# Chunked attention and a bilinear FFN on one core: x columns in token order, output stores of 128 rows, one output chunk in each slot, weight sums moved into later steps

## The chip, the core and the metric

The kernel runs on one core of one Trainium2 chip. The metric is the device time of one execution in microseconds (us); less is better. The kernel before takes 318.6 us, the median of three runs (318.14 to 318.9).

## What is computed

Attention inside chunks of 64 tokens, 8 batches of 8 heads with 576 tokens each and a head size of 64. Its result, 4608 tokens by 512 columns, is x. An FFN follows in which two products of x are multiplied with each other:

```
scores = scale * (q_c @ k_c^T)            # q_c: batch, head, chunk, 64, 64
attn   = exp(scores) / sum(exp(scores))
x      = (attn @ v_c), heads side by side # 4608 x 512
a = x @ w_a                               # w_a: 512 x 1536
b = x @ w_b                               # w_b: 512 x 1536
out = (a * b) @ w_out                     # w_out: 1536 x 512, out: 4608 x 512 float32
```

## The kernel before

**Tiling.** The 4608 tokens are 9 blocks of 512 (K = 0 to 8), each of two units of 256. A unit holds four chunks of 64 tokens in each of its heads. Attention of a unit consists of *scores* (PE L248, then the exponential E on ACT, L256), *sums* (PE L263 multiplies E with ones; ACT takes the logarithm ln, L273), *inverse* (ACT L282, an exponential of -ln) and *values* (PE L296, then DVE L305 multiplies by the inverse and writes fp16 columns of x into the tile xT of the block). q and k are loaded (SP; L188 for the first six units, L176 after, as for v), cast to bf16 (POOL L203) and transposed: units 0 to 5 on PE, with the copy L225 to SBUF on ACT and DVE, later units by DMA (L230).

Within a unit, values computes two tiles of 128 tokens' columns, `av[0]` and `av[1]`. Tile c holds chunk c of token group 0 and chunk c of token group 1. L305 writes tile c into 128 columns that lie together. So the columns of x, and with them the rows of every output tile, stand in the order chunk, group, token, and an output tile of 128 rows covers two runs of 64 tokens in `out` that lie 128 apart.

**Hidden layer.** *Block 0* takes 12 steps of 128 hidden columns for its 512 tokens: PE L355 forms b (bank pb) and a (bank pc or po), ACT L363 copies b to SBUF (tiles b_sb, u_sb, v_sb, c_sb in turn), DVE L364 multiplies the two into ab_sb. *Block 1* does the same in 24 half steps: twelve for unit 2's 256 columns, then twelve for unit 3's (0 to 23); here b goes to pa or pq. *Blocks 2 to 8* use Strassen's scheme in Winograd's form, seven products in place of eight. Each takes six steps (pieces i of 256 hidden columns); a product is four matmuls of 128 x 256 (PE L405). p1 goes into bank pa, ACT L423 copies it into a bank pb, p6 adds to this bank, ACT L416 copies it out as u_sb, p5 adds again, and ACT L416 copies it out as v_sb. p3 of a step, which adds to the same bank, is issued in the *next* step, behind that step's p1. p7 and p4 go to bank pc; DVE adds with L443 and L444 and multiplies with L455.

This needs sums of weights (`combine_w`, DVE L129, four parts for each of six pieces; the list `combos` holds parts 0 to 2 of all pieces, and part 3 overwrites wa, which the steps of block 1 still read), sums of x (`combine_x`, DVE L385, tiles s), sums of w_out (POOL L158) and sums of ab (`combine_ab`, L485, on POOL or DVE, tiles so).

**Output.** Blocks 0 and 1 multiply ab by w_out as it is (PE L605; tiles of 128 rows). Block 0's four tiles stand between half steps of block 1 (`out_0`). Each tile is read out of its bank by DVE L598. Blocks 2 to 8 use the seven products again (class `OutGroup`, PE L543): 14 **chunks** of six matmuls of 128 x 256, two for each product. The chunks of a block run during the next block: a step has two **slots**, one behind p1 and one behind p2, and the table `chunks` says how many run in each. Readouts are L555 to L570 on ACT and L576, L583, L587 on DVE, into tiles o_sb. L576 reads the last product's two chunks out of bank po. L583 and L587 read what the fifth product left.

For the last block two half groups `ends`, one for each half of the rows, run behind the last step's p3 and p4. Their products go in the order 0, 1, 2, 4, 3, 5, 6; their banks are given in a tuple, of which the third is that of the fifth and seventh products.

**Order.** The program's order of code is each engine's order of instructions; an engine runs its own in order and waits at each for the semaphores of others. SP issues loads, transposes and stores in one such queue. PSUM has eight banks: pa, pc, po and pq one each, pb and pt two each. `bank()` without a pool takes the next of the list `spread`. The pool of o_sb has two buffers. `store` (L487 to L491) issues each output tile of 128 rows as two DMAs of 64, on SP; for the last tiles, with `both`, one of the two goes to ACT's queue.

## Time and profile before

| what | us |
|---|---|
| median of three runs | 318.6 |
| the profiled execution, its own time | 317.81 |
| span of its trace | 316.0 |
| of it outside the span | 1.8 |

By stage, the busy time of the engines in the profiled execution, in us:

| stretch | length | PE | DVE | ACT | POOL | DMA share |
|---|---|---|---|---|---|---|
| 0 to 41.6: loads, first units, block 0 | 41.60 | 32.39 | 21.29 | 19.70 | 22.46 | 1.05 |
| 41.6 to 85: block 1 | 43.40 | 41.13 | 33.43 | 22.56 | 22.76 | 1.07 |
| 85 to 115: block 2 | 30.00 | 29.63 | 20.89 | 19.73 | 18.88 | 1.07 |
| 115 to 300: blocks 3 to 8 | 185.00 | 183.18 | 128.24 | 126.42 | 110.57 | 0.57 |

The mean granted clock of TensorE is 0.998. Times in rows of the trace are us from the start of the span. A row of the time order gives start, length, engine, line, operation, output <- inputs, and in brackets the idle time of the engine ahead of it with what ended it. A busy PE is not PE at its peak, since matmuls overlap and their ends are modelled: four matmuls of one product show 0.60, though the next product can start earlier. SPq is SP's queue of DMA issues.

### The profile page before, as it was taken

The numbers are of one execution on the slowest core, as the hardware profiler recorded it, in microseconds if no ns is written. First come the engines' busy times: TensorE is split into PE (matmuls) and PEld (weight loads), VectorE is DVE, ScalarE is ACT, GpSimd is POOL, SyncE is SP. The second block draws the span as 40 slices with busy tenths as digits, with TensorE's granted clock in tenths as the row PEclk, the third lists the DMA queues.
The fourth block names the chain that finished last, engine by engine and source line by source line (L and its number), as shares of the span: only waits on it lengthen the run. The fifth ranks groups of instructions, "written<-read, shape, count | busy, mean of one in ns | idle before, by whom it ended". The sixth has DMA issues, their size and how long they took to land.

```text
span 316.0 us, 8540 instructions
## 1 busy us (share of the span) xinstructions
PE 294.8 (93%) x3476; PEld 228.6 (72%) x3478; DVE 209.6 (66%) x346; ACT 191.8 (61%) x346; POOL 177.6 (56%) x168
## 2 busy tenths in 40 slices
PE   2879999998999999999999999999999999999981
PEld 1534477675576768787888788878887888788871
DVE  3356778965875776578657774877487748847651
ACT  1643666238466566767776668576857685564530
POOL 1575656632646869756945593659356604750830
PEclk9999999999999999999999999999999999999999
DMA  7999999999999984998279838982973002200415
GB/s 233 308 381 292 287 337 310 268 220 183 230 238 223 199 198 100 153 232 218 68 173 187 222 91 191 197 220 66 218 108 77 2 2 66 70 1 2 94 40 133
DMA packets 139495, 54.03 MB, mean 171 GB/s; under 512 B 114624, under 2 KB 133568, under 8 KB 139456
## 3 DMA queue, kind: packets, MB, share of 16 engines
q1 hardware_dynamic: 139296, 53.36, 72.9%
q8 instruction: 27, 0.44, 0.6%
q10 hardware_dynamic: 160, 0.13, 0.1%
q14 instruction: 12, 0.10, 0.1%
HBM read 37.75 MB, written 9.44 MB: 149 GB/s over the span
## 4 chain that ended last, share of the span: by engine, by line
PE 69%; DVE 7%; DMA 7%; POOL 5%; SPq 4%; ACT 4%; issue 3%; POOLq 0%; DVEq 0%; ACTq 0%
PE pb L405 16%; PE pc L405 10%; PE pa L405 9%; PE po L543 9%; PE pq L543 7%; DMA st<-in_q_dram 3%; PE pb L605 3%; SPq L176 2%; DMA st<-in_moe_w_b_dram 2%; ACT E L256 2%; DMA st<-in_v_dram 2%; POOL so L485 2%; PE pt L248 2%; DVE s L385 1%; PE pt L296 1%
## 5 line engine op out<-in xcount | busy, mean ns | idle before, releaser
L405 PEld LDWEIGHTS <-t 128*128 128x128 f16 x504 | 48.3, 98 | 10.6 <-issue 3.8
L485 POOL TENSOR_TENSOR so<-ab_sb 128x512 f16<-128x512 f16 x20 | 23.1, 1154 | 54.7 <-DVE ab_sb L455 54.7
L405 PE MATMUL pb<-s,wa 128*128 128x256 f16 x336 | 50.6, 273 | 1.1 <-ACT v_sb L416 1.1
L443 DVE TENSOR_TENSOR c_sb<-pc,v_sb 128x512 f32<-128x512 f32 x42 | 28.8, 686 | 33.6 <-ACT v_sb L416 32.5
L405 PE MATMUL pa<-xT,wb 128*128 128x256 f16 x336 | 50.4, 273 | 0.0
L416 ACT COPY u_sb<-pb 128x512 f32<-128x512 f32 x42 | 24.7, 587 | 23.0 <-PE pb L405 21.7
L405 PEld LDWEIGHTS <-wa 128*128 128x128 f16 x336 | 30.9, 98 | 7.9 <-issue 2.0
L405 PEld LDWEIGHTS <-wb 128*128 128x128 f16 x336 | 32.9, 98 | 4.0
L543 PEld LDWEIGHTS <-ab_sb 128*128 128x128 f16 x336 | 32.9, 98 | 3.9
L203 POOL CAST k_raw<-st 128x1024 bf16<-128x1024 f32 x17 | 18.1, 1062 | 30.7 <-DMA st<-in_k_dram 30.7
L455 DVE SCALAR_TENSOR_TENSOR ab_sb<-pc,c_sb 128x512 f16<-128x512 f32 x42 | 28.9, 689 | 6.9 <-PE pc L405 5.7
L416 ACT COPY v_sb<-pb 128x512 f32<-128x512 f32 x42 | 24.8, 590 | 14.1 <-PE pb L405 14.1
L455 DVE SCALAR_TENSOR_TENSOR ab_sb<-pb,b_sb 128x512 f16<-128x512 f32 x42 | 28.8, 686 | 6.0 <-PE pb L405 5.5
L423 ACT COPY pb<-pa 128x512 f32<-128x512 f32 x42 | 24.6, 585 | 12.2 <-PE pa L405 12.1
L416 ACT COPY b_sb<-pa 128x512 f32<-128x512 f32 x42 | 25.0, 596 | 6.8 <-PE pa L405 6.8
L444 DVE TENSOR_TENSOR pc<-pc,u_sb 128x512 f32<-128x512 f32 x42 | 28.9, 689 | 0.0
L543 PEld LDWEIGHTS <-so 128*128 128x128 f16 x252 | 24.6, 98 | 4.5 <-DVE so L485 1.4
L203 POOL CAST v_raw<-st 128x1024 bf16<-128x1024 f32 x18 | 18.9, 1052 | 15.3 <-DMA st<-in_v_dram 11.9
L305 DVE TENSOR_TENSOR xT<-pt,ln 128x512 f16<-128x512 f32 x31 | 20.0, 684 | 10.9 <-PE pt L296 10.9
L405 PE MATMUL pb<-s,t 128*128 128x256 f16 x168 | 25.3, 273 | 0.9 <-DVE s L385 0.6
L203 POOL CAST q_raw<-st 128x1024 bf16<-128x1024 f32 x17 | 17.7, 1043 | 14.3 <-DMA st<-in_q_dram 9.8
L405 PE MATMUL pc<-s,t 128*128 128x256 f16 x168 | 25.2, 273 | 0.4 <-DVE ab_sb L455 0.4
(135 smaller groups left out, 580.2 us busy)
## 6 DMA issues: line engine op xcount, KB each, us to landing
out_dram<-o_sb SPq DMA_DIRECT2D x68, 128.0 KB, 2.4
st<-in_v_dram SPq DMA_DIRECT2D x32, 256.0 KB, 4.1
st<-in_q_dram SPq DMA_DIRECT2D x23, 256.0 KB, 4.1
st<-in_k_dram SPq DMA_DIRECT2D x23, 256.0 KB, 3.7
st<-in_moe_w_b_dram SPq DMA_DIRECT2D x6, 512.0 KB, 7.3
st<-in_moe_w_a_dram SPq DMA_DIRECT2D x6, 512.0 KB, 8.0
st<-in_moe_w_out_dram SPq DMA_DIRECT2D x6, 512.0 KB, 6.6
st<-in_q_dram SPq DMA_DIRECT2D x4, 512.0 KB, 4.9
```

What stands on the lines that cost most here:

```text
L176: nc.sync.dma_start(out=st[p:p + n, g], in_=src[b, :, s:s + n, :].rearrange("h p d -> p h d"))
L203: eng.tensor_copy(out=raw[n, U], in_=staged.pop((n, U)))
L305: nc.vector.tensor_tensor(out=x_tiles[K][:, :, c0:c0 + 128], in0=av[cl].rearrange("p m g s -> p m (g s)"), in1=rs[:, cl], op=MULT,)
L405: nc.tensor.matmul(t[:, h * 256:h * 256 + 256], w[:, kt, h * 128:h * 128 + 128], x[:, kt], start=start and h == 0 and kt == 0, stop=h == 1 ...
L416: nc.scalar.copy(out=t, in_=src)
L423: nc.scalar.copy(out=self.B, in_=self.A)
L443: nc.vector.tensor_tensor(out=self.c, in0=self.C, in1=self.v, op=ADD)
L444: nc.vector.tensor_tensor(out=self.C, in0=self.C, in1=self.u, op=ADD)
L455: nc.vector.scalar_tensor_tensor(out=self.dst[:, :, c0:c0 + 256], in0=t.rearrange("p (h n) -> p h n", h=2), scalar=AB_SCALE, in1=o.rearran ...
L485: (eng or nc.gpsimd).tensor_tensor(out=o, in0=x0, in1=x1, op=op)
L543: nc.tensor.matmul(t[:, c0:c0 + 256], a[:, kt, th * 128:th * 128 + 128], w[:, kt], start=n in (0, 4) and first and kt == 0, stop=last and ...
L605: nc.tensor.matmul(out_ps[K, tg], ab_tiles[K][:, ft, tg * 128:tg * 128 + 128], wo_sb[:, ft], start=(ft == 0), stop=(ft == NFT - 1),)
```

## The change

Parts, in the order of the diff:

1. L305 writes each tile's two groups of 64 tokens to where they stand in token order. Each row of 128 columns becomes two runs of 64 with a gap of 64.
2. `store` issues one DMA of 128 rows in place of two of 64. Of the last block's six stores, the one of the last half tile goes to ACT's queue and the other five to SP's.
3. Block 0's output tiles are read out by ACT (L600) in place of DVE.
4. Unit 2's scores, and its sums, inverse and values, stand one step of block 0 later: behind steps 8 and 10 (counted from 0) in place of 7 and 9.
5. Weight sums of the list `combos`: in block 1, half steps 0 to 9 have none (before, 1, 2, 3, 5, 6, 7, 9, 10, 11, 12 and 14 had one); half steps 10 and 11 have one each, and so have unit 3's (12 to 23) except 17, 21 and 23. The part-3 sums, behind half steps 15, 17, 19, 21 and 23, and the seven sums of block 0, behind its steps 3 to 9, stay.
6. At the end of block 1, the values of unit 4 take banks from the longer list `spread`, and the last half step stands behind the values of unit 5 and the sums of x instead of ahead of them.
7. The table `chunks`: blocks 4 to 7 have a chunk in each slot and a second in two; block 8 has one in each of its twelve slots. Its last two chunks of 14, those of the seventh product of block 7's output, run behind the last step, after the sums `combine_ab` of the last block.
8. The first half group of `ends` uses the banks pt, pq, po in place of po, pq, pt.

```diff
         for cl in range(2):
-            c0 = 256 * u + 128 * cl
+            x = x_tiles[K][:, :, 256 * u:256 * u + 256]
             nc.vector.tensor_tensor(
-                out=x_tiles[K][:, :, c0:c0 + 128],
-                in0=av[cl].rearrange("p m g s -> p m (g s)"),
-                in1=rs[:, cl],
+                out=x.rearrange("p m (g c s) -> p m g c s", g=2, c=2)[:, :, :, cl, :],
+                in0=av[cl],
+                in1=rs[:, cl].rearrange("p m (g s) -> p m g s", g=2),
...
-    def store(K, u, c, o_sb, cols=slice(0, DM), both=False):
-        for g in range(2):
-            r0 = K * BLK + 256 * u + 128 * g + 64 * c
-            eng = nc.scalar if both and g else nc.sync
-            eng.dma_start(out=out[r0:r0 + 64, cols], in_=o_sb[g * 64:g * 64 + 64, cols])
+    def store(K, u, c, o_sb, cols=slice(0, DM), eng=nc.sync):
+        r0 = K * BLK + 256 * u + 128 * c
+        eng.dma_start(out=out[r0:r0 + 128, cols], in_=o_sb[:, cols])
...
-                    store(self.K, 1, c, self.o1[:, c], lo if one else slice(0, DM), one)
+                    store(
+                        self.K, 1, c, self.o1[:, c], lo if one else slice(0, DM),
+                        nc.scalar if one and th else nc.sync,
+                    )
...
-        nc.vector.tensor_scalar(out=o_sb, in0=t, scalar1=OUT_SCALE, scalar2=None, op0=MULT)
+        if K == 0:
+            nc.scalar.activation(out=o_sb, in_=t, func=AF.Copy, scale=OUT_SCALE)
+        else:
+            nc.vector.tensor_scalar(out=o_sb, in0=t, scalar1=OUT_SCALE, scalar2=None, op0=MULT)
...
-            if ft == 7:
+            if ft == 8:
                 slot(2)
-            if ft == 9:
+            if ft == 10:
                 slot(None, 2)
...
-            if ft % 4 if u == 0 else ft in (0, 2):
+            if ft > 9 if u == 0 else ft != 5 and ft != 9 and ft != 11:
                 combo()
...
-        spread[:] = [psum_t]
         values(4)
...
         out_0(2)
-        h(1)
         spread[:] = [psum_t]
         values(5)
         combine_x(2)
+        h(1)
         out_0(3)
...
-            4: (0, 1, 1, 1, 2, 1, 2, 2, 1, 1, 1, 1),
+            4: (1, 1, 1, 1, 1, 1, 2, 2, 1, 1, 1, 1),
+            NBLK - 1: (1,) * 12,
...
-            OutGroup(NBLK - 1, 0, (psum_o, psum_q, psum_t)),
+            OutGroup(NBLK - 1, 0, (psum_t, psum_q, psum_o)),
...
             combine_ab(NBLK - 1, 3, j, nc.vector if j == 2 else nc.gpsimd)
+        chunk(2)
```

Three places in the order of instructions follow. Line numbers of the kernel after differ by a few: L541 is L543 of before, L574 is L576, L584 is L583, L588 is L587, L489 is L491.

PE at the start of block 4, before: the product p1 of the first step (bank pa; wb is w_b's piece 0), then p3 of block 3's last step (bank pb; wa is w_a's piece 5, s a sum of x).

```order
L405 LDWEIGHTS wb_186
L405 MATMUL pa<-xT,wb_186 128x256
L405 LDWEIGHTS wa_445
L405 MATMUL pb<-s_2049,wa_445 128x256
L405 LDWEIGHTS wa_445
```

And after, where ab_sb and wo are operands of the first chunk of block 3's output:

```order
L405 LDWEIGHTS wb_186
L405 MATMUL pa<-xT,wb_186 128x256
L541 LDWEIGHTS ab_sb
L541 MATMUL po<-wo,ab_sb 128x256
L541 LDWEIGHTS ab_sb
```

The chunk, six pairs of weight load and matmul of which the fence shows the first, now stands between p1 and p3; the first p3 pair follows it.

DVE at the end of the program, before: the sums of ab of the last piece (so), then the readouts of the last block's half groups into o_sb.

```order
L485 TENSOR_TENSOR ab_sb<-ab_sb 128x2x256
L485 TENSOR_TENSOR so_5440<-ab_sb,so_5311 128x512
L583 SCALAR_TENSOR_TENSOR o_sb<-pt,vo_sb 128x256
L587 TENSOR_TENSOR pt<-pt,uo_sb 128x256
L583 SCALAR_TENSOR_TENSOR o_sb<-pa,v_sb 128x256
L587 TENSOR_TENSOR pa<-pa,u_sb 128x256
L576 TENSOR_SCALAR o_sb<-pt 128x256
L576 TENSOR_SCALAR o_sb<-pa 128x256
```

And after:

```order
L485 TENSOR_TENSOR ab_sb<-ab_sb 128x2x256
L485 TENSOR_TENSOR so_5393<-ab_sb,so_5268 128x512
L574 TENSOR_SCALAR o_sb<-po 128x2x256
L584 SCALAR_TENSOR_TENSOR o_sb<-po,vo_sb 128x256
L588 TENSOR_TENSOR po<-po,uo_sb 128x256
L584 SCALAR_TENSOR_TENSOR o_sb<-pa,v_sb 128x256
L588 TENSOR_TENSOR pa<-pa,u_sb 128x256
L574 TENSOR_SCALAR o_sb<-po 128x256
L574 TENSOR_SCALAR o_sb<-pa 128x256
```

The readout of block 7's seventh product (the row of 128x2x256) has moved from the last step to behind the last sum of ab, and the first half group's rows name po in place of pt.

ACT in steps 8 to 11 of block 0, the piece of the difference: L363 copies b of one step each; E, ln and the inverse (L282) are unit 2's.

```order
 L363 COPY c_sb<-pb 128x512
+L363 COPY b_sb<-pb 128x512
 L256 ACTIVATE E<-pa 128x512
 L256 ACTIVATE E<-pq 128x512
-L363 COPY b_sb<-pb 128x512
 L363 COPY u_sb<-pb 128x512
-L273 ACTIVATE ln<-pt 128x512 x2
-L282 ACTIVATE ln<-ln 128x1024
 L363 COPY v_sb<-pb 128x512
+L273 ACTIVATE ln<-pt 128x512 x2
+L282 ACTIVATE ln<-ln 128x1024
 L363 COPY c_sb<-pb 128x512
```

Unit 2's exponentials stand one copy later, and so do its logarithms and its inverse, which after the change have one copy of block 0 behind them in place of two.

More of the change, by code (lines that the diff above doesn't have):

```diff
@@ L823 @@
                     last.add7()
-                chunk(chunks[min(K, 4)][2 * i])
+                chunk(chunks.get(K, chunks[4])[2 * i])
                 if last:
@@ L832 @@
                 now.p2()
-                chunk(chunks[min(K, 4)][2 * i + 1])
+                chunk(chunks.get(K, chunks[4])[2 * i + 1])
                 attend(K, i, 1)
@@ L838 @@
         ends = [
-            OutGroup(NBLK - 1, 0, (psum_o, psum_q, psum_t)),
+            OutGroup(NBLK - 1, 0, (psum_t, psum_q, psum_o)),
             OutGroup(NBLK - 1, 1, (psum_t, psum_b, psum_a)),
         ]
-        assert not outs
         last.add7()
@@ L850 @@
             combine_ab(NBLK - 1, 3, j, nc.vector if j == 2 else nc.gpsimd)
+        chunk(2)
+        assert not outs
         for n in (1, 2, 4, 3, 5, 6):
```

## Prediction

> **What bounds the kernel now.** I read the page first, then the busy time by stretch, then who waited for whom on PE, then the instructions in order of time at the places these name.
>
> ```profile
> span 316.0 us, 8540 instructions
> PE 294.8 (93%) x3476; PEld 228.6 (72%) x3478; DVE 209.6 (66%) x346; ACT 191.8 (61%) x346; POOL 177.6 (56%) x168
> PE 69%; DVE 7%; DMA 7%; POOL 5%; SPq 4%; ACT 4%; issue 3%; POOLq 0%; DVEq 0%; ACTq 0%
> ```
> ```profile
> 50.00:60.00 10.00, 9.09 (x108) 7.14 (x106) 8.76 (x18) 5.11 (x12) 5.65 (x6) 1.00 1.08 254
> 70.00:80.00 10.00, 9.17 (x135) 5.99 (x133) 5.56 (x12) 7.65 (x14) 2.62 (x3) 1.00 1.16 198
> 300.00:316.00 16.00, 8.47 (x76) 7.06 (x74) 5.78 (x12) 3.41 (x9) 2.89 (x3) 0.96 0.36 88
> ```
>
> In the second fence the columns behind a stretch and its length are the busy time of PE, its weight loads, DVE, ACT and POOL, then granted clock, DMA share and GB/s. PE works 93% of the span and most of the chain runs through it; no other engine comes near. The change adds no product and takes none away. So it can fill gaps of PE, make new ones, or shorten what follows PE's last product. The gaps: some 0.9 us in each ten of block 1 (the stretches from 50 and from 70), a hole at the start of most later blocks, and 7.5 us in the last 16.
>
> **The tail.**
>
> ```profile
> 303.23 0.39 PE L543 MATMUL pq<-wot,so 128*128 128x256 f16 x2 [1.08 <-DVE so L485]
> 303.43 0.41 DVE L485 TENSOR_TENSOR so<-ab_sb,so 128x512 f16<-128x512 f16 x1
> 304.11 0.82 PE L543 MATMUL pt<-wot,ab_sb 128*128 128x256 f16 x6
> 304.77 0.82 PE L543 MATMUL pa<-wot,ab_sb 128*128 128x256 f16 x6
> 297.31 0.69 DVE L576 TENSOR_SCALAR o_sb<-po 128x512 f32<-128x512 f32 x1 [0.40 <-PE po L543]
> 306.69 0.42 DVE L583 SCALAR_TENSOR_TENSOR o_sb<-pt,vo_sb 128x256 f32<-128x256 f32 x1 [2.85 <-ACT vo_sb L566]
> 309.59 0.42 DVE L576 TENSOR_SCALAR o_sb<-pa 128x256 f32<-128x256 f32 x1 [0.23 <-PE pa L543]
> ```
> ```profile
> L491 SPq DMA_DIRECT2D out_dram<-o_sb x10: 466/542/664, 307.1 to 312.9; - x10
> 312.89 0.54 SPq L491 DMA_DIRECT2D out_dram<-o_sb  x1
> out_dram<-o_sb SPq DMA_DIRECT2D x4, 128.0 KB, 2.4
> out_dram<-o_sb SPq DMA_DIRECT2D x6, 64.0 KB, 2.0
> DMA to landing us min/median/max: 1.9/2.4/4.8
> L176 SPq DMA_DIRECT2D st<-in_k_dram x27: 564/585/1852, 63.1 to 223.4; - x27
> ```
>
> A chunk (six products) takes PE 0.66 us, from 304.11 to 304.77. The last two chunks of block 7 leave the steps of block 8 (2 x 0.66 = -1.31) and run behind the last group's product, ahead of the wait of 1.08. Keep a clock on which that product stays where it is. The sum that waited at 303.23 then starts 1.31 later and finds its operand ready. But the next but one, the row at 304.11, now goes into bank po, and that is **a first new wait**: DVE must read the two moved chunks out of po first (L576, 0.69), behind its last L485, which ends at 303.84. So 304.53, with the signal 304.6: +0.5. PE works in order, so what is left of the product waits behind it.
>
> **A second new wait** stands at L583. It overwrites the o_sb buffer that block 7's last two stores read, and these now start on SP only after that readout, at 304.6 and 305.1. Behind L583 on DVE stand the next three operations that PE's sixth sum needs, and both last readouts. These stores carry 256 KB each; no row shows one. From below they land in 2.4 us, as at 128 KB; from above in 4.8, the longest landing of any store. From 64 to 128 KB a landing grows by 0.4; I take 2.65, near the lower rows. The buffer is then free at 305.1 + 2.65 = 307.75, L583 starts there and not at 307.2 (306.69 + 0.5), and the last result, of 310.0 (309.59 + 0.42), comes at 310.6.
>
> What follows weighs most. SP issues ten stores from 307.1 to 312.9, one each 0.6 us: the last starts 2.9 us after the last result and lands 2.0 later, 314.9. With five on SP and one on ACT, SP starts its last at 310.7 and ACT at 310.6. These carry 128 KB in rows of 1 KB: 2.3 to land (bounds 2.0 and 2.4), so 313.0, 1.9 earlier. With the chunks, **-3.2**. An issue should not grow with its rows: L176 issues 128 x 8 pieces in 0.585. Bounds: -3.4 with a landing of 2.4 at the second wait, -1.1 with 4.8.
>
> [...] No run so far shows a 128-row store.
>
> **Starts of blocks 4 to 8.**
>
> ```profile
> 146.43 0.60 PE L405 MATMUL pa<-xT,wb 128*128 128x256 f16 x4
> 147.27 0.60 PE L405 MATMUL pb<-s,wa 128*128 128x256 f16 x4 [0.25 <-ACT v_sb L416]
> PE pb L405 <- ACT v_sb L416: 1.1, 4, 0.3
> 114.47 1.03 PE L605 MATMUL pq<-wo,ab_sb 128*128 128x512 f16 x4
> 115.33 0.60 PE L405 MATMUL pb<-s,wa 128*128 128x256 f16 x4
> 270.63 0.60 PE L405 MATMUL pb<-s,t 128*128 128x256 f16 x4 [0.22 <-ACT pb L423]
> 273.67 0.60 PE L405 MATMUL pc<-s,t 128*128 128x256 f16 x4 [0.44 <-DVE ab_sb L455]
> ```
>
> Four products of this size take 0.44 us start to start (0.66 for six), so behind 146.43 the next could start at 146.87. It starts at 147.27: 0.40 lost where the row calls 0.25 idle, 0.15 more, since ends are modelled. It waits for v_sb on ACT. The third row counts four such waits, 1.1 us idle: 1.1 + 4 x 0.15 = 1.7 lost in blocks 4 to 7. The change puts a chunk of 0.66 into exactly this place, longer than the longest of them (0.3 idle, 0.5 lost). Block 3 already has a chunk there (114.47), and 115.33 shows no wait. The slot that gives its second chunk away keeps one. Block 8 loses 0.22 + 0.44 + 2 x 0.15, about 1.0. Its first wait goes the same way; the second hangs on DVE's sums of x, which stay, so I take 0.6 (bounds 0 and 1.0). In all **-2.3**, bounds -1.7 and -2.7.
>
> **Block 1: where its first x is made.**
>
> ```profile
> 34.12 0.22 PE L248 MATMUL pa<-qkt 64*64 64x64 bf16 x2 [0.26 <-DVE qkt L225]
> 38.06 0.41 PE L263 MATMUL pt<-E,ones 64*64 64x512 bf16 x4
> 41.34 0.68 DVE L305 TENSOR_TENSOR xT<-pq,ln 128x512 f16<-128x512 f32 x1
> 41.62 1.03 PE L355 MATMUL po<-xT,wa 128*128 128x512 f16 x4
> 42.49 0.60 PE L355 MATMUL pa<-xT,wb 128*128 128x256 f16 x4
> ```
>
> From the sums at 38.06 to the end of L305 at 42.02 it is 3.96 us of two logarithms, an exponential and two L305. Two steps of block 0 cover it, 1.73 each (0.87 from 41.62 to 42.49, twice). Moved one step on, the sums come at 38.06 + 1.73 - 0.4 = 39.4 (the wait at 34.12 goes, 0.26 + 0.15). Now x is ready at 43.35 and only one step covers it: sums and values, 0.8, and that step end at 41.9. PE **waits 1.5 us**, and block 1 starts at 43.4 in place of 42.49: +0.95. Bounds: 0, should ACT and DVE be that much faster, which no row suggests, and 1.0.
>
> **Block 1: the weight sums.**
>
> ```profile
> L129 DVE TENSOR_TENSOR wa<-wa,wb x5: 414/514/1240, 61.6 to 81.2; 128x512 f16<-128x512 f16 x5
> 56.35 0.60 PE L355 MATMUL po<-xT,wa 128*128 128x256 f16 x4 [0.49 <-DVE ab_sb L364]
> 60.19 0.60 PE L355 MATMUL po<-xT,wa 128*128 128x256 f16 x4 [0.19 <-DVE ab_sb L364]
> ```
>
> A sum takes DVE 0.41 to 1.24 us; the long ones stand beside a cast on POOL, which is busy 5.65 of the ten from 50. I take the middle, 0.83. They cost PE 0.65 at 56.35, 0.35 at 60.19 and another 0.3 of the 0.91 idle in that ten, 1.3. In the change, half steps 1 to 9 have none, but from half step 10 each has one. From the multiply of half step 10 to that of 14 DVE has four sums and four multiplies (0.41 each, as the sum alone), 4 x 1.24 = 5.0, PE four half steps of 0.87, 3.5. DVE falls 1.5 behind; the two banks let it lag 0.4, and 1.1 is lost, 0.2 less than now. Bounds: 0.3 lost with all sums at 0.41, 2.7 with all at 1.24. Later sums stand where DVE has room (5.56 of the ten from 70).
>
> **Block 1: its end.**
>
> ```profile
> 75.36 0.44 PE L296 MATMUL pt<-E,v_raw 64*64 64x64 bf16 x30 [0.81 <-ACT E L256]
> 84.32 0.57 ACT L423 COPY pb<-pa 128x512 f32<-128x512 f32 x1 [3.57 <-PE pa L405]
> 84.81 1.09 ACT L256 ACTIVATE E<-pt 128x512 bf16<-128x512 f32 x2
> 85.29 0.61 PE L405 MATMUL pb<-s,t 128*128 128x256 f16 x4 [0.63 <-DVE s L385]
> ```
>
> The values of unit 4 get a bank that is free, and the wait of 0.81 goes. Next late is v_sb's copy on ACT, queued behind those same exponentials, for which the following row sums must wait: 0.35 is left of it. At 85.29 half step 23 now covers the sums of x. What is late next there is ACT: an output copy, 0.6, taken over from DVE, now stands ahead of L423 (84.32), and the exponentials (1.09), u_sb and v_sb behind it. This gives back the 0.63 and about 0.5 more before step 1 is through (bounds 0 and 1.0). Block 1: 0.95 - 0.2 - 0.35 + 0.5 = **+0.9**, bounds -0.4 and +2.5.
>
> **What I cost at nothing.**
>
> ```profile
> L305 DVE TENSOR_TENSOR xT<-pt,ln 128x512 f16<-128x512 f32 x31 | 20.0, 684 | 10.9 <-PE pt L296 10.9
> L225 DVE COPY qkt<-pt 128x512 bf16<-128x512 bf16 x10 | 6.7, 721 | 0.0
> ```
>
> L305 now writes runs of 64; L225 writes strided already at nearly the same 0.7. Fewer issues on SP inside the blocks free SP, but who waits on PE there names no DMA.
>
> **Sum.** -3.2 - 2.3 + 0.9 = **-4.6 us**. The profiled execution took 317.8 (span 316.0, 1.8 around it), so 313.2 by its measure. The median shown, 318.6, is 0.8 above it: 318.6 - 4.6 = **314.0**.
>
> **Rivals.** *Block 1 gains:* sums and casts miss each other and ACT keeps up, -0.4: 312.7. For it, DVE idles 4.4 of the ten from 70; against it, the wait for x needs no cast. *The sums pile up,* +2.5: 315.6. For it, DVE is busy 8.76 of the ten from 50. *The stores are no cheaper:* an issue of 128 rows takes 1.2 us, or 256 KB land at 4.8; either leaves about -1.0 of the tail: 316.2. Against it, the L176 row. *The change doesn't do what it says:* the holes at the blocks move along with the chunk and the stores keep their queue, 317.5 to 318.6. Against it, block 3. *Slower:* L305 writes at half its rate, 1.3 us more on DVE in each of 14 units that follow, ahead of the multiplies that PE waits for. Idle time of DVE there hides some 0.8; 14 x 0.5 = 7.0, more than the 4.6: 321.0. It decides from 0.33 exposed a unit. Against it, the L225 row.
>
> **Numbers.** Forecast, 313.1 to 314.9: 0.45; block 1 gains 0.22; pile-up 0.14; stores 0.11; nothing done 0.05; slow L305 0.03. The range 312.0 to 316.3 takes in the first four but for their edges, and leaves out about 0.15. Faster by over 0.2% (0.6 us, about what a measurement of this kernel tells from no change) 0.94, within it 0.03, slower 0.03.
>
> **What would show it.** Right: PE idle about 1.5 us before block 1's first product, ended by xT; no wait for v_sb at the starts of blocks 4 to 7; L583's operation waiting for a store; the last issue within 0.2 us of the last result. Wrong: stores still queued on SP after the last result, an issue of 1 us, L305 over 0.8, or block 1 through earlier than now.

## The result and the profile after

The kernel after takes 310.88 us, the median of four runs (310.62 to 311.0), beside 318.74 for the kernel before in the same session (318.14 to 318.9, four runs). The ratio is 0.9756, with a 95% interval of 0.9739 to 0.9773. The forecast was 314.0, with a range from 312.0: the direction was right, the gain of 7.9 us is 3.3 larger than the 4.6 foretold, and the time lies below the range.

The two profiled executions differ by less than the medians: 317.81 against 310.94, spans 316.0 and 309.1, so 6.9. The 1.0 between 6.9 and 7.9 is taken up below, with the second profile of before.

From the page of the kernel after: the span, busy times by engine, and the shares of the chain of waits.

```profile
span 309.1 us, 8485 instructions
PE 293.2 (95%) x3476; PEld 228.9 (74%) x3478; DVE 205.2 (66%) x342; ACT 194.0 (63%) x350; POOL 178.6 (58%) x168
PE 81%; DVE 6%; ACT 4%; POOL 4%; issue 2%; DMA 2%; SPq 0%; DVEq 0%; POOLq 0%; ACTq 0%
```

SP's queue has left the chain (4% before) and DMA has 2% of it in place of 7%. PE's busy time is about the same, so what went is idle time around it. The view of waits on PE, of the kernel after, names what is left behind the start of block 1 (us in total, times, longest):

```profile
PE pa L355 <- DVE xT L305: 1.5, 1, 1.5
PE pa L263 <- ACT v_sb L363: 0.5, 1, 0.5
PE pc L405 <- DVE ab_sb L455: 0.5, 2, 0.3
PE pb L405 <- ACT pb L423: 0.4, 1, 0.4
...
PE pq L541 <- POOL wo L158: 0.3, 1, 0.3
PE po L541 <- DVE o_sb L574: 0.2, 1, 0.2
```

Gone against before are the waits for ab_sb of L364 (0.7), E (0.8), s (0.6), v_sb of L416 (1.1 in four) and so (1.1), and in block 0 those for qkt of unit 2 (0.3) and its v_raw (0.2). New are xT (1.5), v_sb of L363, L423 in block 2, the sums of w_out and bank po.

The start of the same product in both profiles shows where the time went. Each difference of two shifts is what the stretch between gained:

| product | before | after | shift | of it the stretch's | forecast |
|---|---|---|---|---|---|
| first of block 1 | 42.49 | 43.43 | +0.94 | +0.94 | +0.95 |
| half step 11 (bank po) | 56.35 | 56.35 | 0.00 | -0.94 | with the next |
| half step 21 (bank pq) | 73.36 | 73.00 | -0.36 | -0.36 | -0.2 in both |
| p6 of block 2's step 1 | 89.24 | 88.34 | -0.90 | -0.54 | +0.15 |
| p1 of block 4's first step | 146.43 | 146.14 | -0.29 | +0.61 | 0 |
| p4 of the last step | 299.80 | 295.70 | -4.10 | -3.81, of it two chunks -1.31 and the starts -2.50 | -1.31 and -2.3 |
| last product of all | 308.74 | 305.06 | -3.68 | +0.42 | +0.5 |
| end of the span | 316.0 | 309.1 | -6.9 | -3.2 | -2.4 |

The forecast of the last row is what the prediction's tail of -3.2 leaves beside the chunks and the first new wait: -3.2 + 1.31 - 0.5. The tail gave -1.31 + 0.42 - 3.2 = -4.1, block 1 -0.9 in place of +0.9.

**The tail.** Rows of the kernel after in order of time, then its stores by source line within that stretch, and its DMA issues there with the median time to land:

```profile
299.71 0.68 DVE L574 TENSOR_SCALAR o_sb<-po 128x512 f32<-128x512 f32 x1
300.44 0.81 PE L541 MATMUL po<-wot,ab_sb 128*128 128x256 f16 x6 [0.21 <-DVE o_sb L574]
303.16 0.43 DVE L584 SCALAR_TENSOR_TENSOR o_sb<-po,vo_sb 128x256 f32<-128x256 f32 x1 [2.77 <-DMA out_dram<-o_sb]
305.91 0.42 DVE L574 TENSOR_SCALAR o_sb<-pa 128x256 f32<-128x256 f32 x1 [0.23 <-PE pa L541]
306.37 0.37 ACTq L489 DMA_DIRECT2D out_dram<-o_sb  x1
```
```profile
L489 SPq DMA_DIRECT2D out_dram<-o_sb x7: 332/379/424, 300.4 to 305.7; - x7
```
```profile
out_dram<-o_sb SPq DMA_DIRECT2D x4, 256.0 KB, 2.1
out_dram<-o_sb SPq DMA_DIRECT2D x3, 128.0 KB, 1.7
out_dram<-o_sb ACTq DMA_DIRECT2D x1, 128.0 KB, 1.8
```

Both new waits stand where they were foretold, L574's 0.21 on PE and L584's on a store. L584's costs next to nothing: its other operand, vo_sb, comes at 302.98, 0.18 earlier, and DVE idles again before 305.91. SP starts its last issue at 305.7, ahead of the last result (306.33); ACT's follows that result at once. From last result to end it is 2.8 us, before it was 6.0. An issue takes 0.33 to 0.42 here, before 0.47 to 0.66.

**The start of block 4**, where a chunk now stands behind p1, in order of time:

```profile
146.14 0.60 PE L405 MATMUL pa<-xT,wb 128*128 128x256 f16 x4
146.57 0.82 PE L541 MATMUL po<-wo,ab_sb 128*128 128x256 f16 x6
147.23 0.60 PE L405 MATMUL pb<-s,wa 128*128 128x256 f16 x4
```

146.57 to 147.23 is 0.66, a chunk with no gap behind it: v_sb is there.

**Block 1.** First x, last half steps, and busy time in two of the stretches shown of before:

```profile
42.70 0.68 DVE L305 TENSOR_TENSOR xT<-pq,ln 128x512 f16<-128x512 f32 x1
43.43 0.60 PE L355 MATMUL pa<-xT,wb 128*128 128x256 f16 x4 [1.47 <-DVE xT L305]
76.03 0.40 PE L263 MATMUL pa<-E,ones 64*64 64x512 bf16 x2 [0.47 <-ACT v_sb L363]
84.25 0.60 PE L405 MATMUL pb<-s,t 128*128 128x256 f16 x4 [0.36 <-ACT pb L423]
```
```profile
50.00:60.00 10.00, 9.71 (x117) 8.04 (x116) 6.95 (x17) 5.55 (x13) 5.79 (x6) 1.00 1.05 250
70.00:80.00 10.00, 9.46 (x164) 6.12 (x161) 7.00 (x14) 8.39 (x16) 3.73 (x4) 1.00 1.16 217
```

L305 writes its two runs in 0.68, as before. PE waits 1.47 for it, as foretold. In the ten from 50 DVE's busy time fell from 8.76 to 6.95, and PE's rose from 9.09 to 9.71. The first five weight sums, and the two casts on POOL beside them:

```profile
56.54 0.47 DVE L129 TENSOR_TENSOR t<-t,wb 128x512 f16<-128x512 f16 x1
57.39 0.41 DVE L129 TENSOR_TENSOR t<-wb,t 128x512 f16<-128x512 f16 x1
58.27 0.72 DVE L129 TENSOR_TENSOR t<-wa 128x512 f16<-128x512 f16 x1
59.24 0.41 DVE L129 TENSOR_TENSOR t<-t,wb 128x512 f16<-128x512 f16 x1
60.01 0.81 DVE L129 TENSOR_TENSOR t<-wb,t 128x512 f16<-128x512 f16 x1
57.45 1.26 POOL L203 CAST k_raw<-st 128x1024 bf16<-128x1024 f32 x1 [0.71 <-DMA st<-in_k_dram]
59.30 1.25 POOL L203 CAST v_raw<-st 128x1024 bf16<-128x1024 f32 x1 [0.59 <-DMA st<-in_v_dram]
```

### The profile page after: what moved, and what is told of

Same layout as the page of the kernel before. It is cut to its first block, busy times and chain, and to the rows that moved or that the text cites. A ratio compares the mean times of both kernels' runs of the same rounds, so it can differ in the third digit from the quotient of the medians.

```text
span 309.1 us, 8485 instructions
## 1 busy us (share of the span) xinstructions
PE 293.2 (95%) x3476; PEld 228.9 (74%) x3478; DVE 205.2 (66%) x342; ACT 194.0 (63%) x350; POOL 178.6 (58%) x168
## 4 chain that ended last, share of the span: by engine, by line
PE 81%; DVE 6%; ACT 4%; POOL 4%; issue 2%; DMA 2%; SPq 0%; DVEq 0%; POOLq 0%; ACTq 0%
PE pb L405 17%; PE pc L405 11%; PE pa L405 10%; PE po L541 9%; PE pq L541 8%; PE pb L609 3%; PE pb L355 3%; PE pc L355 3%; PE po L355 3%; DMA st<-in_q_dram 2%; PE pq L355 2%; POOL so L485 2%; PE pa L355 2%; PE pt L296 1%; PE pt L263 1%
## 5 line engine op out<-in xcount | busy, mean ns | idle before, releaser
L416 ACT COPY u_sb<-pb 128x512 f32<-128x512 f32 x42 | 24.7, 587 | 24.8 <-PE pb L405 23.5
L541 PEld LDWEIGHTS <-ab_sb 128*128 128x128 f16 x336 | 32.9, 98 | 4.2 <-issue 0.4
L455 DVE SCALAR_TENSOR_TENSOR ab_sb<-pc,c_sb 128x512 f16<-128x512 f32 x42 | 28.9, 688 | 6.9 <-PE pc L405 5.5
L455 DVE SCALAR_TENSOR_TENSOR ab_sb<-pb,b_sb 128x512 f16<-128x512 f32 x42 | 28.8, 687 | 2.8 <-PE pb L405 2.4
L416 ACT COPY v_sb<-pb 128x512 f32<-128x512 f32 x42 | 24.9, 592 | 8.1 <-PE pb L405 8.1
L423 ACT COPY pb<-pa 128x512 f32<-128x512 f32 x42 | 24.6, 586 | 8.4 <-PE pa L405 8.3
L416 ACT COPY b_sb<-pa 128x512 f32<-128x512 f32 x42 | 25.0, 595 | 7.7 <-PE pa L405 7.7
L305 DVE TENSOR_TENSOR xT<-pt,ln 128x512 f16<-128x512 f32 x30 | 19.4, 684 | 12.2 <-PE pt L296 12.2
L541 PEld LDWEIGHTS <-so 128*128 128x128 f16 x252 | 24.6, 98 | 3.4 <-issue 0.5
```

Of the source, the lines that this page charges most:

```text
L305: nc.vector.tensor_tensor(out=x.rearrange("p m (g c s) -> p m g c s", g=2, c=2)[:, :, :, cl, :], in0=av[cl], in1=rs[:, cl].rearrange("p m ...
L416: nc.scalar.copy(out=t, in_=src)
L423: nc.scalar.copy(out=self.B, in_=self.A)
L455: nc.vector.scalar_tensor_tensor(out=self.dst[:, :, c0:c0 + 256], in0=t.rearrange("p (h n) -> p h n", h=2), scalar=AB_SCALE, in1=o.rearran ...
L541: nc.tensor.matmul(t[:, c0:c0 + 256], a[:, kt, th * 128:th * 128 + 128], w[:, kt], start=n in (0, 4) and first and kt == 0, stop=last and ...
```

## The experiments

All times in us; the ratio is to the kernel before, run in turn on the same chip, with its 95% interval. A blank line divides what ran together on one chip. Executions of one kernel scatter, so a step of less than about 0.5 is read from the traces. The kernel after ran in the second and the fourth group, and with the result; the medians of the first and third group stand beside it across chips, so there the traces decide.

| kernel | median (lowest to highest, runs) | ratio | span of its profile |
|---|---|---|---|
| before | 318.96 (317.67 to 321.21, 13) | | |
| before_again | 320.38 (1) | | 318.6 |
| u_slot | 310.9 (310.38 to 311.57, 4) | 0.9757 (0.9725 to 0.9788) | 308.6 |
| u_sums | 312.27 (311.61 to 312.92, 4) | 0.9799 (0.9767 to 0.983) | 310.0 |
| s_only | 315.69 (314.01 to 318.15, 10) | 0.9893 (0.986 to 0.9925) | 315.0 |
| | | | |
| before | 319.33 (318.12 to 322.47, 11) | | |
| after_again | 310.77 (310.35 to 311.04, 4) | 0.9724 (0.9681 to 0.9766) | 308.7 |
| u_end | 311.28 (310.52 to 313.3, 6) | 0.9751 (0.9711 to 0.9791) | 308.7 |
| u_out0 | 310.72 (310.23 to 310.96, 4) | 0.9721 (0.9679 to 0.9764) | 308.8 |
| split_x | 310.58 (310.42 to 312.02, 6) | 0.9732 (0.9693 to 0.9772) | 308.6 |
| | | | |
| before | 318.88 (317.89 to 321.59, 12) | | |
| u_table | 312.79 (311.98 to 314.17, 4) | 0.9808 (0.977 to 0.9847) | 312.4 |
| u_tail | 312.83 (311.11 to 313.18, 4) | 0.9794 (0.9755 to 0.9834) | 311.3 |
| u_store64 | 316.45 (316.18 to 316.94, 5) | 0.9921 (0.9891 to 0.9951) | 314.5 |
| bank_c | 311.41 (310.53 to 313.21, 6) | 0.9768 (0.9731 to 0.9804) | 308.9 |
| | | | |
| before | 319.38 (318.36 to 319.89, 11) | | |
| after_third | 311.16 (310.28 to 311.87, 5) | 0.975 (0.9726 to 0.9773) | 310.0 |
| wo_early | 311.19 (310.39 to 311.33, 4) | 0.9747 (0.9725 to 0.9769) | 309.4 |
| all_three | 310.3 (309.59 to 313.28, 6) | 0.9737 (0.9703 to 0.977) | 307.8 |

### The stores

**s_only**: the kernel before with parts 1 and 2 of the change alone (L305 in token order, stores of 128 rows).

```diff
...
-        for g in range(2):
...
-            eng.dma_start(out=out[r0:r0 + 64, cols], in_=o_sb[g * 64:g * 64 + 64, cols])
...
+        eng.dma_start(out=out[r0:r0 + 128, cols], in_=o_sb[:, cols])
...
```

> The kernel before with only the columns of x in token order and the stores of 128 rows. Theory (a store of 128 rows is issued in 0.35 to 0.4 us where one of 64 takes 0.55 to 0.6, and lands in 2.0): SP's queue is empty when the last result comes, and the end stands 2.9 to 3.2 us behind the last readout in place of 6.0: 3 less than before, 315.7. Rival (the prediction's step: same issue time per store, five issues fewer, 2.3 to land): 1.9 less, 316.8. Inside the blocks both expect no change of more than 0.2.

It ran 3.3 under the kernel before. Its last result:

```profile
311.82 0.42 DVE L574 TENSOR_SCALAR o_sb<-pa 128x256 f32<-128x256 f32 x1 [0.23 <-PE pa L541]
```

From there, at 312.24, to its end, at 315.0, it is 2.8, as in the kernel after. The stores shorten the end by 3.2 on their own. The rival's 1.9 fell, by the trace. (The prediction's 1.9 holds 0.6 of new waits that this kernel hasn't; its sizes give 2.5 here, which the trace excludes and the median, with runs from 314.0 to 318.2, does not.) The halved number of issues weighs more than their length: by an estimate from this trace's starts, SP's last issue would stand at about 312.0, still ahead of the last result, had each taken 0.6. Up to the last product this profile is 2.2 behind the first profile of before, but 0.3 ahead of the second (before_again, below), which has the same waits.

**u_store64**: the kernel after with each store in two halves of 64 rows again, at the same addresses as the one of 128.

```diff
-        r0 = K * BLK + 256 * u + 128 * c
-        eng.dma_start(out=out[r0:r0 + 128, cols], in_=o_sb[:, cols])
+        for g in range(2):
+            r0 = K * BLK + 256 * u + 128 * c + 64 * g
+            eng = nc.scalar if both and g else nc.sync
+            eng.dma_start(out=out[r0:r0 + 64, cols], in_=o_sb[g * 64:g * 64 + 64, cols])
```

> The kernel after with each store of 128 rows as two of 64, token order kept; of the last block the second of a pair goes to ACT's queue where it did before. Theory (an issue of 64 rows takes longer than one of 128, 0.57 against 0.37, and there are twice as many): the last issue stands 2.5 us or more behind the last result, 3.0 more in all, 313.8. Rival (the issues are alike, 0.4 in this program too, and the gain came from landings): the last issue within 1 us of the last result, 311.5.

It cost 5.6, not 3.0. Of its trace, the stores of the last stretch by source line, then the rows of DVE and PE that wait:

```profile
L491 SPq DMA_DIRECT2D out_dram<-o_sb x14: 466/596/676, 300.8 to 311.4; - x14
```
```profile
305.12 0.42 DVE L583 SCALAR_TENSOR_TENSOR o_sb<-po,vo_sb 128x256 f32<-128x256 f32 x1 [4.30 <-DMA out_dram<-o_sb]
305.93 0.81 PE L543 MATMUL po<-wot,ab_sb 128*128 128x256 f16 x6 [0.94 <-DVE po L587]
```

Issues are at 0.6 again, so the rival falls: from the last result (307.87) to the end it is 6.6, 3.8 more than in the kernel after. The second new wait of the prediction costs another 1.1, by the shift of the products within the tail: four issues stand in a row, block 7's last store lands at 305.0, L583 waits until then, and behind L587 a product of PE for 0.9. The remaining 0.8 (against the profile of after_again) stands ahead of block 4, in waits that come and go (below), and isn't this edit's. With stores of 64 rows the move of two chunks to the tail thus pays a wait of 1.1, half of the 2.1 that the prediction's bound allows it; in the kernel after this wait has no price.

### The two chunks in the tail

**u_tail**: the kernel after with all 14 chunks of block 7 in block 8.

```diff
-            NBLK - 1: (1,) * 12,
+            NBLK - 1: (1, 1, 1, 1, 1, 1, 2, 2, 1, 1, 1, 1),
```

> The kernel after with all 14 chunks of block 7's output inside block 8 (two slots of block 8 take two), none behind its last step. Theory (the prediction: two chunks fill the wait for so of L485, less the new wait on bank po): 1.31 - 0.39 = 0.9 more, 311.7, with the wait of 1.1 for L485 back and that for L574 (0.2) gone. Rival (the two new waits cost as much as the chunks save): 310.8.

Its trace has the wait for so back and none for po:

```profile
301.71 0.39 PE L541 MATMUL pq<-wot,so 128*128 128x256 f16 x2 [1.16 <-DVE so L485]
```

Counted from the start of block 4 (against the profile of after_again, the shift there is +1.56) to the last product (+2.55), it loses 1.0, as the theory has it (0.9). The median is 2.1 higher. In the profile the rest stands ahead of block 4, 0.9 of it at the end of block 2 in the wait that is treated below; the edit changes no instruction there.

**bank_c**: the kernel after with bank pc for the first half group's fifth and seventh products.

```diff
-            OutGroup(NBLK - 1, 0, (psum_t, psum_q, psum_o)),
+            OutGroup(NBLK - 1, 0, (psum_t, psum_q, psum_c)),
```

> The kernel after with the first half group's fifth and seventh products in bank pc in place of po. Theory (PE's last new wait is for bank po alone): the wait of 0.2 for L574 goes, 0.3 to 0.4 less, 310.4. Rival (the second new wait, of L584 on the stores of block 7, decides then): the wait of L584 for a store stays until the same time, and the last readout with it: 310.7 to 310.9.

PE's wait is gone and its last product comes 0.36 earlier than the shift ahead of it. But the span's end gains nothing of that: from the last result (305.74) it is 3.2 to the end, not 2.8. That is neither the theory nor the rival, since the last readout does come earlier. Two stores now come at almost the same time (SP at 305.45, ACT at 305.78) and land at 307.55 and 307.93, 2.1 behind each, where ACT's took 1.8. The median of 311.4 doesn't tell it from the kernel after.

### The first slots

**u_table**: the kernel after with the table of blocks 4 to 7 as before.

```diff
-            4: (1, 1, 1, 1, 1, 1, 2, 2, 1, 1, 1, 1),
+            4: (0, 1, 1, 1, 2, 1, 2, 2, 1, 1, 1, 1),
```

> The kernel after with the table of blocks 4 to 7 as before: no chunk in the first slot, two in the fifth. Theory (the prediction: a chunk behind p1 covers v_sb's copy, 0.4 a block): the four waits for v_sb of L416 are back, 1.1 us by the rows, 1.6 to 1.7 more in all, 312.4. Rival (the holes would move with the chunk, and something else sets the pace of blocks 4 to 7): 310.8 to 311.0.

Its view of waits on PE has the row of the kernel before back, with 1.0 in place of 1.1:

```profile
PE pb L405 <- ACT v_sb L416: 1.0, 4, 0.2
```

From the start of block 4 (shift +1.97 against after_again) to the last product (+3.64) it loses 1.7, the theory's number to 0.1. The median is 2.0 higher.

### Block 1

**u_sums**: the kernel after with the weight sums in the half steps of before.

```diff
-            if ft > 9 if u == 0 else ft != 5 and ft != 9 and ft != 11:
+            if ft % 4 if u == 0 else ft in (0, 2):
```

> The kernel after with one part undone: the weight sums of block 1 in half steps 1 to 14 as before. Theory (the sums were worth 1.3 us, not the 0.2 of the prediction): 1.2 to 1.4 more than after, 312.2, with 0.6 us or more of PE waits for ab_sb of L364 in block 1, as before. Rival (worth 0.2; the gain of block 1 came from the later start or from the copies on ACT): 311.1, with no such waits.

It is 1.4 to 1.5 slower than the kernel after (310.88, 310.77), and its waits on PE have these two rows more:

```profile
PE pc L355 <- DVE ab_sb L364: 0.6, 2, 0.3
PE po L355 <- DVE ab_sb L364: 0.3, 1, 0.3
```

By the shift of the products against after_again it loses 1.3 between the first product of block 1 and half step 22 (+0.04 to +1.31), and nothing before or behind. So the sums were worth 1.3, and not the 0.2.

**u_end**: the kernel after with the end of block 1 as before.

```diff
+        spread[:] = [psum_t]
         values(4)
...
         out_0(2)
+        h(1)
         spread[:] = [psum_t]
         values(5)
         combine_x(2)
-        h(1)
```

> The kernel after with the end of block 1 as before: unit 4's values in the two banks pt again, the last half step ahead of unit 5's values. Theory (this part gained what the traces show between the half steps 22 and the first product of block 2, 0.4 to 0.6): 311.4, with PE's wait of 0.8 for E ahead of L296 and that of 0.6 for s of L385 back, and without the waits for v_sb (0.5) and for L423 (0.4). Rival (the prediction: it costs 0.15 in all, since the copies on ACT give the gain back): 310.7 to 310.9.

The waits of 0.8 for E and 0.6 for s are back, those for v_sb and L423 gone. Between half step 21 and step 1 of block 2 it loses 0.5 against the kernel after; the median is 0.5 higher, though its runs go from 310.5 to 313.3. The theory holds; the prediction's +0.15 had the wrong sign.

**u_out0**: the kernel after with block 0's output read out by DVE.

```diff
-        if K == 0:
+        if K < 0:
             nc.scalar.activation(out=o_sb, in_=t, func=AF.Copy, scale=OUT_SCALE)
```

> The kernel after with block 0's four output tiles read out by DVE again. Theory (the copies on ACT are worth having because DVE is the late one in block 1): 0.3 to 0.8 more than after, 311.4, with new waits for ab_sb of L364. Rival (the prediction: a copy ahead of L423 on ACT costs 0.5): the waits of PE for v_sb (0.5) and for L423 (0.4) shrink, 310.4.

Neither: 310.72, and the wait for L423 goes from 0.4 to 0.3. Who reads out these four tiles is worth nothing. The prediction had put 0.5 on it.

**u_slot**: the kernel after with unit 2's scores, and its sums and values, a step of block 0 earlier, as before.

```diff
-            if ft == 8:
+            if ft == 7:
                 slot(2)
-            if ft == 10:
+            if ft == 9:
                 slot(None, 2)
```

> The kernel after with one part undone: unit 2's scores and its sums, inverse and values stand behind steps 7 and 9 of block 0 again. Theory (the terms add): PE's wait of 1.5 us for xT ahead of block 1 goes, block 1 starts at 42.5 in place of 43.43, and the end keeps it: 0.9 less than after, 310.0. Rival (what comes behind is fixed by loads and POOL): block 1 starts earlier by 0.9, but the waits for wo sums of POOL in block 3 and for casts grow by as much: 310.6 to 310.9.

The wait for xT is gone and block 1 starts at 42.75, 0.8 ahead of after_again, yet the time is the same. Where the kernel before waited 0.18 for unit 2's v, this profile waits 0.51:

```profile
38.91 0.22 PE L296 MATMUL pa<-E,v_raw 64*64 64x64 bf16 x2 [0.51 <-POOL v_raw L203]
```

Of the 0.8, 0.4 is lost at the end of block 2 and 0.3 in block 3, in waits for L455 and for the sums of w_out. That is what the rival said would happen; whether the earlier start brings these waits on is taken up below.

**before_again**: the kernel before, profiled a second time.

> The kernel before, unchanged, profiled a second time. Theory: its executions differ by up to 0.8 us among themselves and the first profile (317.81, span 316.0) caught a quick one; a second profile gives 318.1 to 318.9 with a span of 316.3 to 317.1, and the 0.3 to 1.1 us more stand in PE's waits of block 1 (42 to 85), where weight sums on DVE meet casts on POOL. Rival: profiled executions are that much quicker than plain ones; then the span is 316.0 again, within 0.1, and every PE wait is where it was.

Its span is 318.6, 2.6 above that of the first profile. Its rows in order of time:

```profile
40.08 0.22 PE L296 MATMUL pa<-E,v_raw 64*64 64x64 bf16 x2 [1.33 <-POOL v_raw L203]
115.73 0.60 PE L405 MATMUL pc<-s,t 128*128 128x256 f16 x4 [0.83 <-DVE ab_sb L455]
134.04 1.03 PE L543 MATMUL pq<-wo,so 128*128 128x256 f16 x8 [0.60 <-POOL wo L158]
```

The first profile has 0.18 in place of the 1.33 and neither of the other two waits; these rows make up the 2.6 (1.14 + 1.00 + 0.50 by the shifts of the products). My theory put the excess into the weight sums of block 1; it stands ahead of block 1 and behind it. The rival fell too. The first is a cast on POOL whose load of v comes late in some executions; POOL stands idle 0.62 for that load in the first profile of before, and 0.70 in that of the kernel after. With unit 2 a step later its values stand at 39.65 in place of 38.65, which gives that load 1.0 more: none of the three profiles of the kernel after has this wait. The move is thus an exchange: it adds the wait for xT and takes away one of 0.2 to 1.3. In the four profiles with the early place (before, before_again, s_only, u_slot) block 1 starts at 42.5 to 43.9, in the eleven with the late one at 43.2 to 44.2. This and the time lost in blocks 2 and 3 make u_slot and the kernel after tie; the runs don't tell the two apart.

**split_x**: the kernel after with unit 2's sums and inverse behind step 9 and its values behind step 10.

```diff
+            if ft == 9:
+                sums(2)
+                inverse(2)
             if ft == 10:
-                slot(None, 2)
+                values(2)
```

> The kernel after with unit 2's sums and inverse one step of block 0 earlier (behind step 9) and its values where they are (behind step 10). Theory (the wait of 1.5 us for xT is the chain of two logarithms and an exponential; ahead of the values it is covered, and the late load of v stays covered too): the wait goes, 1.3 to 1.5 less than after, 309.5. Rival (the later work of block 1 and 2 is tied to POOL and the loads): the wait goes but its time comes back in block 1 to 3 as waits for POOL or DVE, 310.4 to 310.9.

The wait for xT falls from 1.5 to 0.6 only: ACT's copy v_sb stands behind the inverse, a multiply on DVE waits 1.3 for that copy, and both L305 stand behind the multiply. 310.58 can't be told from 310.77. Its profile has the waits for L455 and for the sums of w_out at the end of blocks 2 and 3 (0.3 each), which that of after_again, with the later start, has not: the rival's case, to which the next part turns.

### Why time gained in block 1 is partly lost in blocks 2 and 3

Between step 1 of block 2 and block 4 the kernel after lost 0.61: 0.42 at the end of block 2, and 0.20 in block 3, where PE waits for a sum of w_out. Its rows at the first of the two places, DVE's sums of x for block 3 beside POOL's sum of w_out, and PE behind them:

```profile
110.70 0.46 DVE L385 TENSOR_TENSOR s<-xT 128x512 f16<-128x512 f16 x1
111.19 1.26 DVE L385 TENSOR_TENSOR s<-s,xT 128x512 f16<-128x512 f16 x1
110.84 1.33 POOL L158 TENSOR_TENSOR wot<-wo,wot 128x512 f16<-128x512 f16 x1
113.11 0.60 PE L405 MATMUL pc<-s,t 128*128 128x256 f16 x4 [0.25 <-DVE ab_sb L455]
```

**after_again** and **after_third** are the same kernel in other sessions, each the reference of the runs beside it.

> The kernel after, unchanged, on the chip of the next three runs, as their reference. All theories: 310.6 to 311.1. If its waits in block 3 (L455 0.3, the sums of w_out 0.3) come and go between its profiles, they are not the change's but a matter of when loads arrive.

> The kernel after, unchanged, as the reference of the next two. 310.6 to 311.1 if its executions stay as narrow as on two chips before; a wider spread, with waits for L455 at the end of block 2, if they are a matter of when loads arrive.

The same rows of after_again, then those of after_third:

```profile
111.04 0.41 DVE L385 TENSOR_TENSOR s<-xT 128x512 f16<-128x512 f16 x1
111.49 0.42 DVE L385 TENSOR_TENSOR s<-s,xT 128x512 f16<-128x512 f16 x1
```
```profile
110.60 1.11 DVE L385 TENSOR_TENSOR s<-xT 128x512 f16<-128x512 f16 x1
111.74 1.26 DVE L385 TENSOR_TENSOR s<-s,xT 128x512 f16<-128x512 f16 x1
113.66 0.60 PE L405 MATMUL pc<-s,t 128*128 128x256 f16 x4 [1.02 <-DVE ab_sb L455]
```

So these waits come and go between executions. In after_again POOL's casts in block 2 come some 2 us earlier than in the first profile, its sum of w_out is through at 111.14, and DVE's second sum starts behind it. In after_third POOL is late, with two sums of ab and that of w_out in a row from 110.27 to 114.02, and both of DVE's meet them. What PE loses there goes with the sum of the two durations, over all 17 profiles: nothing in the eight where it is at most 1.2, 0.4 to 0.5 in the four with 1.7 to 1.8, 0.8 to 1.4 in the five with 2.1 to 2.7. after_third passed block 1 0.6 earlier than after_again and ended 1.2 later. The 0.61 is therefore no property of the change. Nor does the start of block 1 alone decide it: u_tail and u_table start it 0.5 later than after_again and lose 0.9 and 1.4.

**wo_early** moves one of POOL's sums out of the last step of block 2; **all_three** joins it with split_x and bank_c.

```diff
-                    for _ in range(2 if i < 3 else 1):
+                    for _ in range((3, 2, 2, 1, 1, 0)[i]):
```

> The kernel after with one sum of w_out on POOL moved from the sixth step of block 2 to its first, so that POOL has none where DVE makes the sums of x of L385 for block 3. Theory (those two sums take 1.26 each beside POOL's L158 and 0.42 alone, and PE then waits for L455): both L385 there take 0.5 or less, the wait for L455 of 0.2 to 1.2 at the end of block 2 is gone in every execution, 0 to 0.4 less than the reference and no run above 311.1. Rival (POOL's other sums, of ab, come to stand there, or the wait follows the loads alone): L385 still 0.9 or more in the profile, same time and spread as the reference.

> The kernel after with that sum moved, with unit 2's sums and inverse one step earlier and with the first half group's bank pc in place of po. Theory (each took a wait of PE away, and without the meeting of DVE and POOL in block 2 the time of the earlier two is kept): block 1 starts 0.5 to 0.9 earlier, PE ends 0.3 earlier in the tail, 309.6 to 309.9. Rival (block 1's time is given back in blocks 2 and 3 whatever POOL does there): 310.3 to 310.7.

In both profiles DVE's sums are shorter than in after_third, though one of wo_early's takes 0.74 and not the 0.5, and the wait at the end of block 2 is gone; wo_early's rows, then those of all_three:

```profile
111.52 0.74 DVE L385 TENSOR_TENSOR s<-xT 128x512 f16<-128x512 f16 x1
112.29 0.43 DVE L385 TENSOR_TENSOR s<-s,xT 128x512 f16<-128x512 f16 x1
```
```profile
110.10 0.42 DVE L385 TENSOR_TENSOR s<-xT 128x512 f16<-128x512 f16 x1
110.55 0.42 DVE L385 TENSOR_TENSOR s<-s,xT 128x512 f16<-128x512 f16 x1
```

wo_early's profile waited 1.1 for the cast of k in block 0, and its median is the reference's; its highest run is 311.3 against 311.9, too little to call, and above the 311.1 expected. So what the meeting costs is shown, and not that this edit avoids it: in after_third DVE's sums start beside POOL's sums of ab, which wo_early leaves in place. all_three's profile keeps the earlier start of block 1 to the end (shift -0.78 there, -1.33 at the last product, against after_again; 0.37 of this is bank_c's and, as there, is gone at the end of the span). Its median is 0.9 under after_third's and its lowest run, 309.59, is the lowest of all; but it also has a run of 313.28, and the two intervals overlap. Whether it beats the kernel after stays open.

## Why the prediction was wrong

The four parts, by its own steps, in the profile that it was made against:

- **Starts of blocks 4 to 8, -2.3: right.** -2.5 in the trace, and u_table undoes four of them for 1.7.
- **The chunks and both new waits: right.** -1.31 and +0.42 (forecast +0.5); L584 waits for a store, 0.18 past its other operand, and the end does not feel it (forecast 0.1, bound 2.1). In u_store64 it costs 1.1.
- **Block 1's first x, +0.95: right** as a wait (1.47, +0.94). What it missed is the other side: the row "PE pa L296 <- POOL v_raw" with 0.2 stood in the trace, the wait varies from 0.2 to 1.3 over the profiles with the early place, and the move covers it.
- **The stores, -2.4: too small by 0.8.** The step that failed is the landing of the last store: it took 2.3, between bounds of 2.0 and 2.4 that both come from stores of 64 rows, and ACT's store of 128 rows landed in 1.8. That is 0.5. The rest is 0.1 each for the last issue, which follows the result at once, for the second wait, and for the time behind the last landing (1.0 in place of 1.1). An issue did not grow with its rows, as the prediction said; it shrank, to 0.38, which no range had room for. But in the prediction's own sum SP's last issue stands only 0.1 behind the last result, so this is worth little here.
- **The weight sums, -0.2: this step failed, by 1.1.** It took 0.83 for each of four sums, the middle of the two ends, and had PE lose 1.1. In the trace the first five take 0.47, 0.41, 0.72, 0.41 and 0.81, which is 0.56 on average, DVE gets from the multiply of half step 10 (56.21) to that of 14 (59.67) in PE's own 3.5, and the view of waits has none for L364. The lower bound was wrong by its own sum: four sums and four multiplies at 0.41 make 3.3, less than the 3.5, so nothing is lost and not 0.3. The present cost of 1.3 was sized right: u_sums pays it again.
- **The end of block 1, +0.15: this step failed, by 0.7.** Its first half held: up to block 2's first product this stretch gains 0.41 (forecast 0.35). The second failed. It took the output copy on ACT to give back all of the wait for s and 0.5 more; behind that first product the stretch gains another 0.13. The wait for L423 is 0.36, and u_out0 shows that the copy has at most 0.1 of it.
- **Blocks 2 and 3, nothing: +0.6 in this profile,** from the meeting of DVE and POOL. Set against after_again, after_third loses 1.8 there; the second profile of before loses 1.5 against the first.
- **The base.** The sum was taken off a median of 318.6 as if the profile were typical. It is one of the quickest executions of its kernel (317.81; medians of 11 to 13 runs are 318.9 to 319.4). before_again holds waits that the profile lacks: 1.1 for the cast of v, which the move of unit 2 takes away, and 1.5 in blocks 2 and 3, which come and go in the kernel after too. The 1.0 between the difference of the profiles and that of the medians comes from this quick execution; how much of it is the wait that the change removes is not shown.

With the sizes of the stores (-0.8), the sums (-1.1) and the end of block 1 (-0.7), less the 0.6, the -4.6 become -6.6, near the 6.9 of the profiles. The rival *block 1 gains* was the nearest (312.7): it named the sums and casts that miss each other, with block 1 at -0.4. It measured -0.9.

## What to carry to other kernels

Take the price of a wait that ends on a load or on another engine's cast from more than one execution: one profile shows one arrival, and a change that gives the load more time can be worth part of the spread (here the wait was 0.2 in one profile and 1.3 in the next), which a single trace shows as nothing. When a DMA's shape changes, its issue and its landing are unknown on both sides (here the median issue went from 0.60 to 0.42), so let the range hold a gain too. And count a move of work to the tail together with the stores that must leave a buffer there: with stores of 64 rows the wait for that buffer costs 1.1 (u_store64), as much as the move saves (1.0 in u_tail); with the larger stores, which save 3.2 by themselves, it costs nothing.

## What the runs showed of the hardware

- **A store of 128 rows is issued faster than one of 64.** In the tail SP takes 0.33 to 0.42 for 128 rows of 1 or 2 KB, and 0.47 to 0.68 for 64 rows of either (the kernel after against u_store64); over the whole program the medians are 0.42 and 0.60.
- **In the tail it also landed sooner for its size.** There 256 KB from 128 rows land in 2.1 (the kernel after), where 128 KB from 64 rows took 2.4 (before). Over the whole program the medians are 3.4 for 256 KB (after) and 2.4 for 128 KB (before).
- **A sum on DVE of operands in SBUF (L129, L385) takes 0.41 alone and up to 1.41 beside a sum on POOL (u_table).** In the kernel after five such sums that start while a cast or a sum of POOL runs (56.54, 58.27, 60.01, 61.08 and 111.19) take 0.47, 0.72, 0.81, 1.27 and 1.26, and each ends 0.27 to 0.28 behind that operation. The multiplies of L364 at 57.93 and 59.67, which read one operand from PSUM, stand inside casts too and take 0.42. The sums at 57.39 and 59.24 start 0.06 ahead of a cast and keep their 0.41, and the two casts take 1.26 and 1.25 in place of 1.04.
- **Executions of one program differ by when a cast behind a load gets done,** which makes 1.1 of the 2.6 between the two profiles of before. The cast of v that unit 2 waits for ends at 38.6 in the first, where PE waits 0.18 for it; in the second PE waits 1.33 for it, until 40.08. Executions of the kernel before ran from 317.7 to 322.5 in five sessions, those of the kernel after from 310.3 to 311.9 in three.
